# Batch 0's q in four loads instead of two, issued first, in a linear-attention and channel-mix kernel; the written order of all pieces is new

## The chip, the cores and the metric

The kernel runs on one core of a Trainium2 chip. The metric is device time in microseconds (us) of one execution. Five engines work side by side, each through its own instruction stream in order: TensorE (PE in the profile, its weight loads PEld), VectorE (DVE), ScalarE (ACT), GpSimd (POOL) and SyncE (SP). POOL and SP here mostly issue DMAs; sixteen DMA engines move the data.

## The reference

Two stages follow each other, with B = 8 batches, H = 8 heads, S = 576 tokens, head size 64, C = 512 channels and F = 1024:

```python
kv = np.einsum('bhsd,bhse->bhde', k, v)          # 64 x 64 for each batch and head
out = np.einsum('bhsd,bhde->bhse', q, kv)
rms = np.sqrt(np.mean(out * out, axis=-1, keepdims=True) + 1e-06)
x = out / rms * g_norm                           # heads side by side: (B, S, C)

x_prev = x shifted by one token (zeros first)
xk = mu_k * x + (1 - mu_k) * x_prev
xr = mu_r * x + (1 - mu_r) * x_prev
k = np.maximum(xk @ w_k, 0)                      # (S, F)
v = k * k @ w_v                                  # (S, C)
return sigmoid(xr @ w_r) * v
```

All inputs and the output are float32 in HBM; the kernel computes in bfloat16 with float32 sums.

## The kernel before, in words

Attention goes batch by batch. For batches 0 and 1 it goes in two halves of four heads (z = 0, 1), which have their own loads and their own kv; from batch 2 on, both halves go together (written 01). Channel mix goes over groups g = 0 to 8 of 512 tokens, which cut across batches: group g needs the batches whose tokens it holds.

The work is cut into pieces. Each piece is a function that issues a few instructions on one engine; the string ORDER (line 16) names every piece once, in the order in which they are issued, and `Plan.emit` runs through it. An engine executes its pieces strictly in that order; semaphores hold a piece back until what it reads is there and until the buffer that it writes is free. Buffers of a kind rotate (for instance 3 for k, v and q each, 4 double banks of PSUM). `@A` and `@D` behind a name choose ACT or DVE where a piece can run on either. The names that matter (b a batch, z a half, i a half of the tokens or of the sequence, g a group):

- `ld.k/v/q b.z`: loads on POOL's queue, which turn float32 into bfloat16 (lines 217 to 230); `ld.wk0/wk1`, `ld.wr`, `ld.wv0/wv1`: the weights (line 252). `ldh.k`, `ldh.v`: k and v of batch 0's first half as float32 on SP's queue (line 236), which `cst` pieces cast.
- `kv b.z` (line 265): k times v on TensorE; `kc`, `ks`, `kd`: copy, a product with a permutation matrix (`perm`) and a second copy, which bring kv into the shape for the next step.
- `tq b.z.i` (line 358): DVE transposes a half of q; `u b.z.i` (line 282): q times kv. In q's tile a row holds 36 tokens, the halves i = 0 and 1 being the first and the last 18 of each row; each `u` piece waits for both transposes of its half of the heads.
- `sq`, `ss`, `rs` (lines 379 to 439): square, mean over a head by a matmul, 1/sqrt; `sp`: SP spreads that over partitions with small DMAs (line 430); `uc`, `mul` scale u; `d`, `mk`, `mr`, `xk`, `xr` form the difference to the token before and the two blends.
- `k g.f`, `relu`, `ksq`, `r g.c`, `sig`, `v g.c.p`, `out`, `st` (lines 454 to 584): the channel mix and the stores. Group 0 starts in quarters, `k0.half i z`.
- `z:512`: a matmul on zeros, which only fills TensorE's time; there are 29 of them and `zz`; 16 and `zz` stand in front of kv0.0.
- `seta`, `setp`, `setb`, `perm`, `ident`, `small`, `tr9`, `cols`: constants and the three small vectors.

A load piece on POOL stands at one place of the order and waits there for its buffer. Loads go out one behind the other, and POOL's rows show waits that pair each load from the ninth on with the landing of the eighth before it.

Of the kernel before, what the change touches and what calls it, by code (L numbers as in the profile page):

```python
# [31 lines left out]
class Plan:  # L32
# [3 lines left out]
    def add(self, name, on, fn, deps=(), bufs=(), also=None):  # L36
        assert name not in self.pieces, name
        p = self.pieces[name] = Piece(name, on, fn, deps, bufs, also)
        return p
# [17 lines left out]
def kernel(  # L57
# [13 lines left out]
    nc = tc.nc  # L71

    B, H, S, HD = q.shape
# [8 lines left out]
    QJ = S // QP  # L82
# [34 lines left out]
    add = plan.add  # L117

    def get(buf, dtype=None):
        if buf.t is None:  # L120
            n, shape, dt = BUFS[buf.tag]
            pool = psum if buf.tag == "ps" else sb
            buf.t = pool.tile(list(shape), dt, tag=buf.tag, name=buf.tag, bufs=n)
        return buf.t
# [24 lines left out]
    cols = const.tile([128, 9], FP32, name="cols")  # L149
    ones = const.tile([128, 128], BF16, name="ones")  # L150
    heads = const.tile([128, 32], BF16, name="heads")
    perm = const.tile([128, 2, 2, 128], BF16, name="perm")
# [8 lines left out]
    kvq = {(n, b): Buf(n) for n in "kvq" for b in range(B)}  # L161
# [37 lines left out]
    def make_cols(_):  # L199
# [12 lines left out]
                deps=[p_ident, p_small], bufs=[ps9])  # L212
    p_cols = add("cols", "D", make_cols, deps=[p_tr9], bufs=[ps9])

    loaded = {}

    def load(b, n, zs):
        def fn(_):
            if n == "q":
                part = slice(64 * zs[0], 64 * zs[-1] + 64)  # L220
                nc.gpsimd.dma_start(out=get(kvq[(n, b)])[part], in_=q[b].rearrange("h s d -> (h s d)").rearrange(  # L221
                    "(p f) -> p f", p=128)[part])
                return
            view = {"k": k, "v": v}[n][b].rearrange("(m e) (p j) d -> (e p) m (j d)", e=2, j=NJ)
            m = slice(2 * zs[0], 2 * zs[-1] + 2)
            nc.gpsimd.dma_start(out=get(kvq[(n, b)])[:, m, :], in_=view[:, m, :])  # L226

        p = add(f"ld.{n}{b}." + "".join(map(str, zs)), "P", fn, bufs=[kvq[(n, b)]])
        for z in zs:
            loaded[(n, b, z)] = [p]  # L230
# [101 lines left out]
    def attention(b):  # L332
        kin, vin, qin = (kvq[(m, b)] for m in ("k", "v", "q"))
        kv, qT = Buf("kv"), Buf("qT")
        bufs = [{t: Buf(t) for t in ("uT", "sq", "rs", "d")} for z in range(NZ)]
# [4 lines left out]
        for zs in zss:  # L340
# [12 lines left out]
            for i in range(2):  # L353
                def tq(_, i=i, part=part):
                    src = qin.t.bitcast(FP32).rearrange("q (a b i) -> q a b i", b=2, i=32)
                    dst = get(qT).rearrange("q a p b r -> q (a p b r)").bitcast(FP32).rearrange("q (a p b) -> q a b p", p=32, b=2)
                    js = slice(QJ // 4 * i, QJ // 4 * i + QJ // 4)
                    nc.vector.transpose(out=dst[part, js], in_=src[part, js])  # L358

                ts.append(add(f"tq{name}.{i}", "D", tq, deps=sum((loaded[("q", b, z)] for z in zs), []), bufs=[qin, qT]))  # L360
            for z in zs:
                qd[z], kvcs[z] = ts, c
        us = [[Buf("ps") for i in range(2)] for z in range(NZ)]
# [259 lines left out]
```

## Time and profile before

| | us |
|---|---|
| median of the 3 timed runs | 199.68 (199.62 to 199.98) |
| the profiled execution | 200.13 |
| its span | 198.4 |
| TensorE busy | 188.4 |
| DVE busy | 137.8 |
| ACT busy | 121.8 |
| last matmul ends | 194.4 |

The span is what the profile covers of the profiled execution; its own time is 1.7 us more. In the timeline a row has a start, a duration, the engine, the line of the kernel, the instruction, what it writes and reads, and how many were merged; in brackets stands how long the engine had been idle before and what ended that. In the rows of DMA queues q0 is the queue of POOL's loads and q1 that of SP; a row has packets, MB and the share of sixteen engines. MB and KB of POOL's loads are counted in bfloat16, as written.

### The profile page before, as it was taken

The numbers are of one execution on the slowest core, as the hardware profiler recorded it, in microseconds if no ns is written. First come the engines' busy times: TensorE is split into PE (matmuls) and PEld (weight loads), VectorE is DVE, ScalarE is ACT, GpSimd is POOL, SyncE is SP. The second block draws the span as 40 slices with busy tenths as digits, with TensorE's granted clock in tenths as the row PEclk, the third lists the DMA queues.
The fourth block names the chain that finished last, engine by engine and source line by source line (L and its number), as shares of the span: only waits on it lengthen the run. The fifth ranks groups of instructions, "written<-read, shape, count | busy, mean of one in ns | idle before, by whom it ended". The sixth has DMA issues, their size and how long they took to land.

```text
span 198.4 us, 4225 instructions
## 1 busy us (share of the span) xinstructions
PE 188.4 (95%) x1735; PEld 93.3 (47%) x1760; DVE 137.8 (69%) x235; ACT 121.8 (61%) x158; POOL 23.7 (12%) x42
## 2 busy tenths in 40 slices
PE   7889989999999999999999999999999999999992
PEld 2445844443544544444358644444444444444451
DVE  2669998897959968998968497899659421520641
ACT  3365499949976689945778986882219840433410
POOL 7743442141313010000000000000000000000000
PEclk9999999999999999999999999999999999999998
DMA  6999999999999999999703511743213000310444
GB/s 223 191 202 214 204 201 207 214 206 216 206 235 264 216 235 272 260 240 256 210 3 88 175 72 56 220 112 78 45 47 111 2 3 0 140 71 0 153 167 160
DMA packets 21032, 30.63 MB, mean 154 GB/s; under 512 B 1932, under 2 KB 14484, under 8 KB 21012
## 3 DMA queue, kind: packets, MB, share of 16 engines
q0 software_dynamic: 11280, 16.19, 45.7%
q1 hardware_dynamic: 9588, 14.03, 22.2%
q8 instruction: 14, 0.23, 0.4%
q10 hardware_dynamic: 144, 0.13, 0.2%
q14 instruction: 6, 0.05, 0.1%
HBM read 33.56 MB, written 9.44 MB: 217 GB/s over the span
## 4 chain that ended last, share of the span: by engine, by line
PE 68%; DMA 26%; POOL 2%; issue 2%; DVE 0%; POOLq 0%
PE ps L554 27%; PE ps L507 24%; DMA v<-in_v_dram 19%; PE ps L534 12%; DMA w_v<-in_moe_w_v_dram 7%; PE ps L282 2%; PE ps L265 1%; PE ps L388 1%; POOL w_k L252 1%; POOL q L221 1%; PE ps L271 0%; POOL k L226 0%; POOL perm L189 0%; POOL v L226 0%; DVE out L581 0%
## 5 line engine op out<-in xcount | busy, mean ns | idle before, releaser
L554 PE MATMUL ps<-w_v,sqk 128*128 128x512 bf16 (+1 forms) x286 | 65.7, 373 | 0.9 <-issue 0.6
L507 PE MATMUL ps<-xk,w_k 128*128 128x512 bf16 (+1 forms) x280 | 58.1, 355 | 1.1 <-issue 0.8
L465 ACT ACTIVATE relu<-ps 128x1024 bf16<-128x1024 f32 x36 | 36.5, 1026 | 32.5 <-PE ps L507 28.8
L554 PEld LDWEIGHTS <-sqk 128*128 128x128 bf16 x296 | 27.8, 98 | 32.2 <-issue 2.5
L507 PEld LDWEIGHTS <-w_k 128*128 128x128 bf16 x288 | 27.5, 98 | 26.7 <-issue 1.4
L567 DVE TENSOR_TENSOR out<-ps,sig 128x1024 f32<-128x1024 f32 x16 | 19.4, 1221 | 21.9 <-PE ps L554 12.5
L534 PE MATMUL ps<-w_r,xr 128*128 128x512 bf16 x139 | 33.6, 379 | 0.3
L522 DVE TENSOR_TENSOR sqk<-relu 128x1024 bf16<-128x1024 bf16 x32 | 21.2, 684 | 10.0 <-ACT relu L465 9.7
L544 ACT ACTIVATE sig<-ps 128x1024 bf16<-128x1024 f32 x18 | 18.2, 1024 | 12.4 <-PE ps L534 11.5
L534 PEld LDWEIGHTS <-xr 128*128 128x128 bf16 x144 | 13.9, 98 | 16.3 <-issue 0.5
L379 ACT ACTIVATE sq<-ps 128x576 bf16<-128x576 f32 x32 | 19.9, 652 | 1.8 <-PE ps L282 1.5
L358 DVE STREAM_TRANSPOSE qT<-q 128x576 f32<-128x576 f32 (+1 forms) x20 | 14.7, 760 | 2.4 <-DMA q<-in_q_dram 2.3
L144 ACT ACT_TABLE_LOAD x12 | 15.4, 1283 | 0.9 <-PEq L607 0.7
L136 DVE TENSOR_SCALAR uT<-ps,cols 128x576 bf16<-128x576 f32 x13 | 10.4, 816 | 7.7 <-ACT sq L379 5.5
L136 DVE TENSOR_SCALAR md<-d,cols 128x576 bf16<-128x576 bf16 x44 | 13.8, 365 | 0.4
L134 ACT ACTIVATE uT<-ps,cols 128x576 bf16<-128x576 f32 x15 | 10.9, 742 | 2.9 <-PE ps L282 2.9
L300 DVE TENSOR_TENSOR d<-xT 128x1152 bf16<-128x1152 bf16 (+1 forms) x18 | 12.3, 689 | 0.4
L313 DVE TENSOR_TENSOR xr<-md,xT 128x1152 bf16<-128x1152 bf16 x14 | 10.4, 750 | 1.6 <-ACT md L134 1.4
L405 DVE TENSOR_TENSOR xT<-uT,rs 128x1152 bf16<-128x1152 bf16 x14 | 10.4, 750 | 1.1 <-ACT rs L288 0.6
L313 DVE TENSOR_TENSOR xk<-md,xT 128x1152 bf16<-128x1152 bf16 x14 | 10.4, 754 | 0.6 <-ACT md L134 0.4
L450 PE MATMUL ps<-zero 128*128 128x512 bf16 x28 | 9.4, 481 | 1.5 <-DVE zero L164 1.2
L282 PE MATMUL ps<-qT,kv 32*64 32x288 bf16 x256 | 8.5, 290 | 0.8 <-DVE qT L358 0.8
(53 smaller groups left out, 120.9 us busy)
## 6 DMA issues: line engine op xcount, KB each, us to landing
out_dram<-out SPq DMA_DIRECT2D x35, 256.0 KB, 2.3
v<-in_v_dram POOLq DMA_DIRECT2D x6, 576.0 KB, 22.9
k<-in_k_dram POOLq DMA_DIRECT2D x6, 576.0 KB, 23.2
q<-in_q_dram POOLq DMA_DIRECT2D x6, 576.0 KB, 25.5
rs<-rsc SPq DMA_DIRECT2D x48, 72.0 KB, 3.2
q<-in_q_dram POOLq DMA_DIRECT2D x4, 288.0 KB, 10.3
w_k<-in_moe_w_k_dram POOLq DMA_DIRECT2D x2, 512.0 KB, 11.4
w_v<-in_moe_w_v_dram POOLq DMA_DIRECT2D x2, 512.0 KB, 13.8
```

Of the source, the lines that this page charges most:

```text
L136: nc.vector.tensor_scalar(out=dst, in0=src, scalar1=col, scalar2=None, op0=ALU.mult)
L144: nc.scalar.preload_act_table_set(name)
L313: nc.vector.tensor_tensor(out=dst[:, 2 * z:2 * z + 2, r0:r0 + w], in0=md.t[:, :, cs], in1=xT[:, :, cur], op=ALU.add)
L358: nc.vector.transpose(out=dst[part, js], in_=src[part, js])
L379: sq_ = add("sq" + name, "A", lambda _, ps=ps, sq=sq, cs=cs, w=w: nc.scalar.activation(out=get(sq)[:, :, cs], in_=ps.t[:, :, 0:w], func=AF ...
L465: nc.scalar.activation(out=get(rt), in_=ps.t, func=AF.Relu)
L507: nc.tensor.matmul(get(ps)[:, fc % 2, a0:a1], w_k_sb[:, cc, 128 * fc:128 * fc + 128], xk[:, cc, x0:x0 + a1 - a0], start=(cc == 0), stop=(c ...
L522: nc.vector.tensor_mul(out=get(sqk)[:, 2 * f2:2 * f2 + 2, :], in0=rt.t, in1=rt.t)
L534: nc.tensor.matmul(get(ps)[:, ci % 2, :], xr[:, cc, n0:n0 + 128], w_r_sb[:, cc, :], start=(cc == 0), stop=(cc == NHP - 1))
L544: nc.scalar.activation(out=get(sg), in_=ps.t, func=AF.Sigmoid)
L554: nc.tensor.matmul(get(ps)[:, bank, cs], sqk.t[:, fc, 128 * ci:128 * ci + 128], w_v_sb[:, fc, cs], start=(fc == 0), stop=(fc == NFC - 1))
L567: dv = add(f"out{g}.{c2}", "D", lambda _, ps=ps, sg=sg, ot=ot: nc.vector.tensor_mul(out=get(ot), in0=ps.t, in1=sg.t), deps=ms + [sg_done], ...
```

## The change

Batch 0's two loads of q (one for each half of the heads) become four: `ld.q0.z` brings the first 18 tokens of each row and `ld.q0.zb` the last 18. Each transpose of batch 0 waits for the load of its own half alone. q0.0, q0.0b and q0.1b are the first loads, ahead of `perm` and `ident`; q0.1 follows k of the second half. The whole order is new, with 34 pieces on another engine; the number of pieces is otherwise the same.

The order is one line in the code; it is wrapped here and cut to the start, the stretch with the later loads, the place around kv7.01, and the end:

```diff
-ldh.k ldh.v seta setp perm ld.q0.0 ld.q0.1 ld.v0.1 ld.k0.1 ld.wk0 ident ld.wk1 ld.v1.1 ld.k1.1 ld.q1.1 ld.wr ld.q1.0 ld.v1.0 ld.k1.0 ld.wv0 ld.wv1
-ld.v2.01 ld.k2.01 ld.q2.01 table small zz cst.k0@D cst.k1@A setb cst.v0@A cst.v1@D tq0.0.1 tq0.0.0 z:512 z:512 z:512 z:512 z:512 z:512 z:512 z:512
-z:512 z:512 z:512 z:512 z:512 z:512 z:512 z:512 kv0.0 tq0.1.0 kc0.0@A z:512 z:512 ks0.0 tr9 cols kd0.0@A u0.0.0 sq0.00 z:512 z:512 z:512 ss0.00 u0.0.1
-rs0.00 mul0.00 d0.00 tq0.1.1 z:512 z:512 kv0.1 ld.k3.01 ld.v3.01 ld.q3.01 sq0.01 kc0.1@A ss0.01 rs0.01 ks0.1 kd0.1@A z:512 z:512 z:512 u0.1.0 sq0.10
-xk0.00 z:512 z:512 z:512 ss0.10 mul0.01 d0.01 xk0.01 rs0.10 mul0.10 d0.10 u0.1.1 k0.000 sq0.11 ss0.11 rs0.11 k0.110 xk0.10 k0.100 mul0.11 k0.001 d0.11
-xk0.11 relu0.00 xr0.11 xr0.00 k0.010 k0.011 kv1.1 ksq0.00 k0.111 kc1.1@A tq1.1.0 tq1.1.1 ks1.1 xr0.10 relu0.01 kd1.1@A relu0.11 ksq0.11 k0.101 xr0.01
-u1.1.1 uc1.11@A sq1.11 u1.1.0 sq1.10 uc1.10@D relu0.10 ksq0.10 r0.0 r0.1 ss1.2 ss1.3 rs1.2 rs1.3 mul1.1 kv1.0 ld.k5.01 ld.v5.01 kc1.0@D tq1.0.1
-tq1.0.0 r0.2 r0.3 sig0.0 ks1.0 kd1.0@A ksq0.01 sig0.1 v0.0.0 u1.0.1 uc1.01@D u1.0.0 v0.1.0 sq1.00 sq1.01 uc1.00@D v0.1.1 d1.1 ss1.1 rs1.1 v0.0.1
-out0.0 ss1.0 rs1.0 v0.2.0 v0.2.1 mul1.0 d1.0 mk1.0@D xk1.0 v0.3.0 v0.3.1 out0.1 mk1.1@A kv2.01
...
+ldh.k ldh.v ld.q0.0 ld.q0.0b ld.q0.1b seta setp ident perm ld.k0.1 ld.q0.1 ld.v0.1 ld.wk0 ld.v1.1 ld.wk1 ld.k1.1 ld.q1.1 ld.k1.0 ld.v1.0 ld.wr ld.q1.0
+ld.wv0 ld.wv1 ld.k2.01 ld.v2.01 ld.q2.01 table small zz setb cst.k0@D cst.v0@D cst.k1@A cst.v1@A z:512 z:512 z:512 z:512 z:512 z:512 z:512 z:512 z:512
+z:512 z:512 z:512 z:512 z:512 z:512 z:512 kv0.0 kc0.0@A z:512 z:512 ks0.0 kd0.0@A tq0.0.0 tq0.0.1 z:512 z:512 u0.0.1 u0.0.0 tr9 sq0.00 cols tq0.1.1
+z:512 z:512 ss0.00 tq0.1.0 rs0.00 mul0.00 d0.00 xk0.00 z:512 z:512 z:512 z:512 kv0.1 ld.k3.01 ld.v3.01 ld.q3.01 sq0.01 ss0.01 kc0.1@A rs0.01 ks0.1
+kd0.1@A z:512 z:512 z:512 u0.1.0 sq0.10 u0.1.1 sq0.11 k0.000 mul0.01 d0.01 xk0.01 xr0.01 ss0.10 rs0.10 mul0.10 d0.10 xk0.10 ss0.11 rs0.11 mul0.11
+k0.010 k0.100 k0.001 relu0.00 k0.011 relu0.01 d0.11 xk0.11 xr0.11 kv1.1 kc1.1@D k0.101 ks1.1 kd1.1@A tq1.1.0 tq1.1.1 relu0.10 k0.110 u1.1.0 ksq0.00
+u1.1.1 sq1.10 xr0.10 uc1.11@A kv1.0 ld.k5.01 ld.v5.01 kc1.0@A uc1.10@D sq1.11 xr0.00 tq1.0.0 k0.111 relu0.11 ss1.3 rs1.3 tq1.0.1 ss1.2 ks1.0 ksq0.11
+r0.2 r0.3 rs1.2 r0.0 mul1.1 kd1.0@A u1.0.1 u1.0.0 sig0.1 sq1.00 r0.1 ksq0.10 sq1.01 uc1.01@A sig0.0 v0.1.0 d1.1 ksq0.01 v0.0.0 v0.0.1 mk1.1@D xk1.1
+ss1.1 uc1.00@D v0.1.1 out0.0 rs1.1 ss1.0 rs1.0 v0.3.0 v0.3.1 v0.2.0 v0.2.1 mul1.0 d1.0 mk1.0@D kv2.01
...
```

From kv2.01 to kv4.01:

```diff
-kv2.01 ld.v4.01 ld.k4.01 ld.q4.01 xk1.1 kc2.01@A mr1.1@A k1.0.0 k1.1.0 ks2.01 k1.2.0 k1.3.0 k1.2.1 kd2.01@A tq2.01.1 tq2.01.0 ld.q6.01 k1.3.1 relu1.1
-k1.0.1 u2.01.1 sq2.11 mr1.0@D k1.1.1 uc2.01@D k1.6.0 k1.7.0 k1.6.1 relu1.0 uc2.11@D u2.01.0 sq2.01 sq2.10 sq2.00 uc2.10@D k1.7.1 k1.4.0 k1.5.0 xr1.1
-k1.4.1 uc2.00@A ss2 kv3.01 ld.k7.01 ld.v7.01 xr1.0 rs2 ksq1.0 kc3.01@D relu1.3 tq3.01.0 tq3.01.1 ld.q5.01 k1.5.1 relu1.2 ksq1.3 r1.0 ks3.01 kd3.01@A
-r1.2 ksq1.1 ksq1.2 r1.1 sig1.0 r1.3 sig1.1 u3.01.0 sq3.00 v1.2.0 uc3.00@D v1.3.0 v1.2.1 sq3.10 u3.01.1 uc3.11@A uc3.10@D kv5.01 ld.k6.01 ld.v6.01
-sq3.11 kc5.01@A v1.3.1 v1.1.0 ks5.01 kd5.01@A v1.1.1 uc3.01@A v1.0.0 sq3.01 ss3 v1.0.1 sp2.0 sp2.1 rs3 st0.0 mul2.0 d2.0 mk2.0@D xk2.0 mul2.1 d2.1
-mk2.1@D st0.1 sp3.0 mr2.0@A xk2.1 k2.2 sp3.1 out1.0 k2.3 out1.1 st1.3 k2.0 kv4.01
...
+kv2.01 ld.k4.01 ld.v4.01 ld.q4.01 kc2.01@A xk1.0 k1.0.0 k1.6.0 mr1.0@A out0.1 k1.7.0 k1.6.1 ks2.01 kd2.01@A tq2.01.0 tq2.01.1 ld.q5.01 k1.7.1 xr1.0
+relu1.3 k1.1.0 k1.0.1 u2.01.1 sq2.11 uc2.01@D k1.2.0 k1.1.1 uc2.11@D sq2.01 relu1.0 k1.3.0 mr1.1@D xr1.1 k1.2.1 u2.01.0 sq2.00 k1.3.1 uc2.00@D ksq1.3
+k1.4.0 k1.5.0 sq2.10 tq3.01.0 relu1.1 ksq1.1 tq3.01.1 k1.4.1 ksq1.0 ss2 rs2 uc2.10@A sp2.1 k1.5.1 relu1.2 r1.2 kv3.01 ld.v6.01 ld.k7.01 ld.q6.01
+kc3.01@A r1.0 r1.3 sig1.1 ks3.01 kd3.01@D ksq1.2 r1.1 sig1.0 v1.1.0 u3.01.1 sq3.11 uc3.11@D sq3.01 v1.0.0 sp2.0 uc3.01@A v1.1.1 u3.01.0 sq3.10 sq3.00
+v1.3.0 uc3.00@A v1.0.1 mul2.1 st0.3 uc3.10@A v1.2.0 kv5.01 ld.k6.01 ld.v7.01 ss3 d2.1 mk2.1@D xk2.1 v1.3.1 mul2.0 d2.0 st0.2 rs3 sp3.0 v1.2.1 mk2.0@D
+xk2.0 kc5.01@A mr2.0@A sp3.1 mr2.1@A ks5.01 kd5.01@D k2.4 k2.5 out1.1 st1.2 xr2.0 k2.2 relu2.2 k2.0 k2.1 ksq2.2 xr2.1 relu2.0 kv4.01
...
```

Around the same amount of TensorE work in both, before and after:

```diff
-r3.2 r3.3 xk4.1 tq6.01.1 sig3.1 v3.2.0 u5.01.1 uc5.01@A v3.2.1
...
+u5.01.1 uc5.11@A uc5.01@A out2.0 st2.0 xr3.0 st2.1 sq5.01 k3.6 k3.7 st1.1 sq5.11 k3.0 relu3.3 st1.0 ksq3.1 u5.01.0 uc5.10@A sq5.10 tq6.01.1 k3.1
+relu3.0 st2.3 r3.0 ksq3.3 r3.1 sig3.0 k3.4 ksq3.0 k3.5 v3.0.0 kv7.01 relu3.2 uc5.00@D kv6.01 sq5.00 ss5 kc6.01@A mul4.1 d4.1 mk4.1@D rs5 v3.1.0
+kc7.01@A ksq3.2 v3.1.1
...
```

The end, and the code:

```diff
-v8.0.10 out8.00 v8.3.00 v8.3.10 out8.30 st8.00 st8.30 v8.3.01 v8.3.11 out8.31 st8.31
+v8.0.10 out8.00 st8.00 v8.2.10 out8.20 st8.20 v8.1.10 out8.10 st8.10 v8.3.01 v8.3.11 out8.31 st8.31 v8.3.00 v8.3.10 out8.30 st8.30
```

```diff
@@ -225,6 +225,15 @@
             m = slice(2 * zs[0], 2 * zs[-1] + 2)
             nc.gpsimd.dma_start(out=get(kvq[(n, b)])[:, m, :], in_=view[:, m, :])
 
+        if n == "q" and not b:
+            def half(_, i):
+                rows_ = slice(64 * zs[0], 64 * zs[0] + 64)
+                src, fs = q[b].rearrange("h s d -> (h s d)").rearrange("(p f) -> p f", p=128), slice(QJ // 2 * HD * i, QJ // 2 * HD * (i + 1))
+                nc.gpsimd.dma_start(out=get(kvq[(n, b)])[rows_, fs], in_=src[rows_, fs])
+
+            loaded[(n, b, zs[0])] = [add(f"ld.{n}{b}.{zs[0]}{x}", "P", lambda _, i=i: half(_, i), bufs=[kvq[(n, b)]])
+                                 for i, x in enumerate(("", "b"))]
+            return
         p = add(f"ld.{n}{b}." + "".join(map(str, zs)), "P", fn, bufs=[kvq[(n, b)]])
         for z in zs:
             loaded[(n, b, z)] = [p]
@@ -357,7 +366,8 @@
                     js = slice(QJ // 4 * i, QJ // 4 * i + QJ // 4)
                     nc.vector.transpose(out=dst[part, js], in_=src[part, js])
 
-                ts.append(add(f"tq{name}.{i}", "D", tq, deps=sum((loaded[("q", b, z)] for z in zs), []), bufs=[qin, qT]))
+                ts.append(add(f"tq{name}.{i}", "D", tq, deps=sum((loaded[("q", b, z)][0 if b else i:][:1] for z in zs), []),
+                              bufs=[qin, qT]))
             for z in zs:
                 qd[z], kvcs[z] = ts, c
         us = [[Buf("ps") for i in range(2)] for z in range(NZ)]
```

## The prediction

> **What bounds the kernel now.** First the page's busy line and its DMA slices, then the TensorE timeline, the issues on POOL with their landing times, and the two DMA queues in short windows.
>
> ```profile
> PE 188.4 (95%) x1735; PEld 93.3 (47%) x1760; DVE 137.8 (69%) x235; ACT 121.8 (61%) x158; POOL 23.7 (12%) x42
> ...
> DMA  6999999999999999999703511743213000310444
> ```
>
> TensorE works without a real gap from about 17 us to its end at 194.40, and the DMA engines are full until about 98 us: the loads of all eight batches stand in one long queue. So there are two clocks to beat, TensorE's sum of matmuls and the arrival of the loads. The timeline shows where they meet:
>
> ```profile
> 9.82 0.44 PE L282 MATMUL ps<-qT,kv 32*64 32x288 bf16 x8 [0.59 <-DVE qT L358]
> ...
> 12.74 0.76 PE L265 MATMUL ps<-v,k 64*64 64x64 bf16 x36 [0.42 <-ACT sq L379]
> ...
> 40.67 0.78 PE L265 MATMUL ps<-v,k 64*64 64x64 bf16 x72
> ...
> 58.89 0.77 PE L265 MATMUL ps<-v,k 64*64 64x64 bf16 x72 [0.35 <-DMA v<-in_v_dram]
> ...
> 94.71 1.03 PE L554 MATMUL ps<-w_v,sqk 128*128 128x512 bf16 x4
> ...
> 101.82 0.78 PE L265 MATMUL ps<-v,k 64*64 64x64 bf16 x72
> ```
>
> In order these are u0.0.0, kv0.1, kv2.01, kv5.01, v3.2.0 and kv6.01 (in the same view kv0.0 starts at 7.29 and k0.000 at 17.01). kv5.01 waits openly for a load. The last loads are issued and land thus (the last column of a load's own line is us from issue to landing):
>
> ```profile
> 59.99 0.74 POOL L226 DMA_DIRECT2D k<-in_k_dram  x1 [4.24 <-PE ps L265]
> ...
> 63.53 0.82 POOL L226 DMA_DIRECT2D v<-in_v_dram  x1 [2.80 <-DMA v<-in_v_dram]
> ...
> v<-in_v_dram POOLq DMA_DIRECT2D x1, 576.0 KB, 31.6
> ...
> q<-in_q_dram POOLq DMA_DIRECT2D x1, 576.0 KB, 26.6
> ```
>
> The second-last load, issued at 63.53, lands at 95.1; q7, issued at 71.97, at 98.6. Before, nothing on TensorE asks for that second-last load until 101.82.
>
> **The change part by part, from the profiled execution (200.13 us, span 198.4; 0.45 above the median of the timed runs, 199.68).**
>
> *Issues.* POOL now waits 1.08 us for the zeroed perm and spends 0.82 on it before the first q, at 2.32. After, three q pieces come first, at about 0.75 (SP and ACT start at 0.74). A q issue took 0.54 us for 288 KB and for 576 KB, so I take 0.54 for a half: three make 1.6, then ident and perm 1.0, so perm is ready at about 3.4; its first reader, ks0.0, runs at 8.51. The two extra issues (1.1 us of POOL) are hidden: each later load waits for the landing of the eighth load before it (the waits named in POOL's rows pair off so), with eight in the queue.
>
> *Landings.* The loads land in issue order. Issue plus time to landing gives the old landings, which I carry over by the bytes up to each load's end: 8.3 us at 0.29 MB (q0.0, 2.32 + 6.0), 9.8 at 0.59, 11.2 at 0.88, 12.75 at 1.18 (k0.1, 4.24 + 8.5), 15.2 at 1.70, 19.4 at 2.52. kv0.1 needed k0.1 as the fourth load, 12.75; now it needs v0.1, with the same bytes before it: 12.75 again. wk1 goes from 18.35 to 19.4, wr from 24.8 to 28.4 (r0.2 comes at about 29). Half of q0.0 should land at about 7.4, the other at 8.4.
>
> *u of the first half.* u0.0.0 waited 0.59 for the transposes (two of 0.75 from 8.34). Now the transposes end near 9.1, and kd0.0 (8.96 + 0.37) binds: u may start at 9.4. But u0.0.1 is put first (0.36), so u0.0.0 ends at 10.15 against 10.26: gain 0.1. mul0.00 stays at 12.1 to 12.2.
>
> *DVE.* setb (1.0 us) moves into DVE's 3.05 us of idle before k lands. tq0.1.0 and tq0.1.1 go into DVE's 1.41 us of idle before mul0.00; tq0.1.0 waits for q0.1 (11.2), with mul0.00 queued behind it, which isn't ready before 12.1 anyway. mul0.01 moves from 15.24 to about 14.5. There xr0.01 (0.95) is put ahead of mul0.10, which waits for ss0.10, now behind k0.000: xk0.10 ends at about 20.0 (before: 19.82).
>
> *TensorE to kv1.1.* kv0.1 to u0.1.0 took 2.37 us (12.74 to 15.11) and still does; u0.1.1 follows with no zeros between, so k0.000 starts at 15.6 to 15.9, not 17.01. Then two ss and two more k0 pieces (0.91 each, 4.57/5) end at 19.1, and k0.001 waits for xk0.10 until 20.0. Its head start of 1.3 is thus mostly idle: with two more k0 pieces kv1.1 comes at 21.9, one k0 piece poorer than before at 22.90. Gain 0.1.
>
> *To kv2.01.* The same pieces precede kv2.01 in both orders. Its later load (v2 now, k2 before) is the seventeenth by bytes and landed at 40.6, so it cannot start before 40.7: nothing gained. For a loss I take 0 to 0.5 (kc1.1 on DVE now stands behind xr0.11).
>
> *40 to 94 us.* TensorE's busy time in windows of 10 us was 9.60, 9.01, 9.84, 9.95, 9.95; 9.95 is what a full one shows, so 1.4 us of idle lies here. The new order puts more in front of kv5.01 (3.5 us, less v1.2.1 at 0.9), so the wait for v5 goes. I credit none to all of the 1.4. One new wait lies here: tq3.01.0 is put ahead of ksq1.1 and ksq1.0 on DVE, which gets there near 50 and waits for q3 (29.74 + 22.1 = 51.85); v1.1.0 on TensorE reads those products, ready at 54.7 (two transposes and two products of 0.7 each); TensorE gets there at 54.1 (13.4 us of matmuls behind 40.7): 0 to 0.6, inside that idle.
>
> *kv7.01, where it ends up.* The pieces ahead of kv7.01 after are those ahead of v3.2.0 before, plus u5.01.0, u5.01.1 (0.38 each) and v3.0.0 (0.86), minus r3.2 and r3.3 (0.86 each): 0.1 less. So at the old pace kv7.01 comes at 94.6, and up to 1.4 earlier if the idle goes. It needs v7, now the second-last load, with the same 0.59 MB behind it: 95.1, and 0.2 from landing to matmul as at kv5.01 (34.52 + 24.2 = 58.7, started 58.89): 95.3. TensorE stops for 0.7 to 2 us, and whatever was won earlier goes into that wait. Queued behind it are kv6.01 (its k6 is earlier, at 90.1), ss5 and v3.1.0; ACT waits for ss5 and kv6.01, DVE has the blends of batch 4 to do. What lies behind it is the same amount: 194.40 - 94.6 = 99.8 us with 0.5 of idle in it. The stores ahead of this point are eleven in both, so I see no reason for another landing; bounds 94.4 and 96.3, since about 0.45 MB of stores moved after 95 us.
>
> *Engines swapped.* 34 pieces change between DVE and ACT (DVE 40 to 36, ACT 40 to 44). A blend product costs 1.43 as a pair on ACT and 0.65 on DVE. Cover: both have idle in every 10 us beyond 100 but one (DVE 9.75 at 130 to 140). Without it one pair costs 0.8; bounds -0.5 (the idle left behind kv7.01) to +0.8; I take 0. *Tail:* the last store goes out on SP instead of ACT; SP's of that size landed in 1.8 us; -0.2 to +0.2, taken 0.
>
> Sum: 95.3 - 94.6 = +0.7, span 199.1, profiled execution 200.85, against the median 200.4.
>
> **The unknown at the start.** Do the earlier q pieces delay k and v of batch 0, on the other queue? Windows 4.5 to 5.0 and 5.0 to 5.5:
>
> ```profile
> q1 hardware_dynamic: 88, 0.19, 98.3%
> q0 software_dynamic: 2, 0.01, 10.5%
> ...
> q0 software_dynamic: 17, 0.08, 90.5%
> q1 hardware_dynamic: 61, 0.08, 42.1%
> ```
>
> q's first packets run 2.2 to 2.7 us after the issue, just when k and v end. Now they could run from about 3.0 to 3.4, with 0.7 MB of k and v still to move. Other rows show how a newcomer fares, between 50 and 96 us with loads and behind 100 without:
>
> ```profile
> out_dram<-out SPq DMA_DIRECT2D x11, 256.0 KB, 7.8
> ...
> rs<-rsc SPq DMA_DIRECT2D x24, 72.0 KB, 6.1
> ...
> out_dram<-out SPq DMA_DIRECT2D x24, 256.0 KB, 2.1
> ...
> rs<-rsc SPq DMA_DIRECT2D x24, 72.0 KB, 2.1
> ```
>
> Even 72 KB waits 4 us behind what the engines hold of the other queue. So k and v, there first, should go first: 0. The other end, equal turns: 1.7 us of k and v take twice that, v lands 1.6 later, kv0.0 at 8.9, ss0.00 and its four zeros push kv0.1 to 13.9, and kv2.01 is 1.2 late. The nearest row is rs, so I take 0 and keep 1.2.
>
> The Trainium skill, "DMA: Bandwidth & Descriptors", section "Queues, rings and completion order", says the opposite: an engine takes turns between queue rows, a whole packet of descriptors at a time. By it the sum would go by equal turns, to 200.9 at most. The 4 us of the rs rows speak against short turns.
>
> **Rivals.** *A, the wait at kv7.01:* +0.7, 200.4 (200.1 to 200.9), 0.45. *B, equal turns at the start:* 1.2 late at kv2.01; if the 1.4 of idle behind it takes nothing up, kv7.01 comes at 95.8, behind v7: 200.9; with a stall of an engine swapped, 201.7. For it: q's early readiness; against: rs. 0.20. It is the case for the skill's rule. *C, faster:* v7 lands before TensorE asks. This decides at a landing of 94.4: if the store traffic goes behind it so that it lands at 93.6, kv7.01 starts at 93.8, and 0.8 of the old idle is kept: 198.9. For: 1.4 of idle is there to win; against: a full DMA queue with the same bytes. 0.17. *D, no change:* landing near 94.8 or the later idle won back: 199.7, 0.18. That the two transposes still wait for both halves (the change not doing what it says) moves u0.0.1 by nothing, since kd0.0 binds.
>
> **Numbers.** Likeliest A: 200.4. 0.2% (0.4 us) is about what a measurement can tell. Faster is C, 0.17; same is D and the edge of A, 0.20; slower is B and the rest of A, 0.63. The range 199.2 to 201.6 leaves out the far half of C and the end of B.
>
> **What would show it.** Right: a wait on a DMA of v in front of kv7.01 near 95 us; kv2.01 at 40.7 to 41.2; u0.0.1 near 9.4; k0.001 idle before 20. Wrong: kv0.0 clearly behind 7.3 (B); kv7.01 without a wait, or v7 landing before 94.4 (C).

## The result and the profile after

The changed kernel takes 199.39 us (median of 21 runs, 199.08 to 199.91) against 199.74 us before on the same chip (21 runs, 199.42 to 200.55): a ratio of 0.998, 95% interval 0.9971 to 0.9989. It is about 0.35 us faster, where 0.7 us slower was forecast. Two more measurements on other chips gave 0.9983 (0.9971 to 0.9995) and 0.9992 (0.998 to 1.0005). The profiled execution took 199.39 us with a span of 197.5, against 200.13 and 198.4 before.

The busy line and the DMA slices of the page after. TensorE has the same work and the same share, DVE is 3.8 us lighter and ScalarE 5.2 us heavier than before, as the swapped pieces say.

```profile
PE 188.0 (95%) x1736; PEld 93.2 (47%) x1760; DVE 134.0 (68%) x227; ACT 127.0 (64%) x166; POOL 24.6 (12%) x44
...
DMA  6999999999999999999632404413506003002226
```

The TensorE timeline after (start, us, engine, line, operands; in brackets the idle time in front and what ended it). Lines of the code stand 9 or 10 further down than before: L274 is kv, L291 u, L418 ss, L492 k0, L517 k.

```profile
7.24 0.76 PE L274 MATMUL ps<-v,k 64*64 64x64 bf16 x36
...
9.34 0.69 PE L291 MATMUL ps<-qT,kv 32*64 32x288 bf16 x16
...
12.01 0.76 PE L274 MATMUL ps<-v,k 64*64 64x64 bf16 x36
...
17.37 0.41 PE L418 MATMUL ps<-sq,ones 128*128 128x288 bf16 x2 [0.83 <-ACT rs L297]
18.25 3.65 PE L492 MATMUL ps<-xk,w_k 128*128 128x256 bf16 x32 [0.48 <-DVE xT L411]
...
40.00 0.78 PE L274 MATMUL ps<-v,k 64*64 64x64 bf16 x72
...
60.07 0.78 PE L274 MATMUL ps<-v,k 64*64 64x64 bf16 x72
63.96 4.49 PE L517 MATMUL ps<-xk,w_k 128*128 128x512 bf16 x20 [0.70 <-DVE xk L322]
...
94.27 1.53 PE L274 MATMUL ps<-v,k 64*64 64x64 bf16 x144
```

These are kv0.0, both u of the first half, kv0.1, ss0.11, a run of k0 pieces, kv2.01, kv5.01, k2.4 and, last, kv7.01 with kv6.01. Two things differ from the forecast. kv0.1 and kv2.01 come 0.73 and 0.67 us earlier than before (12.74 and 40.67). And the row of kv7.01, where the forecast put a wait of 0.7 us, names no wait at all. POOL's issue of v7 and its time to landing, after:

```profile
62.60 0.80 POOL L226 DMA_DIRECT2D v<-in_v_dram  x1 [0.69 <-DMA k<-in_k_dram]
...
v<-in_v_dram POOLq DMA_DIRECT2D x1, 576.0 KB, 28.5
```

It lands at 62.60 + 28.5 = 91.1, not at 95.1, 3.2 us before TensorE asks. From the start of kv0.0 to the end of the last matmul TensorE takes 186.58 us (7.24 to 193.82), before 187.11 (7.29 to 194.40).

### The profile page after: what moved, and what is told of

Its sections match the earlier page's. It is cut to its first block, busy times and chain, and to the rows that moved or that the text cites. A ratio compares the mean times of both kernels' runs of the same rounds, so it can differ in the third digit from the quotient of the medians.

```text
span 197.5 us, 4233 instructions
## 1 busy us (share of the span) xinstructions
PE 188.0 (95%) x1736; PEld 93.2 (47%) x1760; DVE 134.0 (68%) x227; ACT 127.0 (64%) x166; POOL 24.6 (12%) x44
## 4 chain that ended last, share of the span: by engine, by line
PE 73%; DMA 14%; DVE 6%; ACT 2%; issue 2%; SPq 1%; POOL 0%; DVEq 0%; ACTq 0%
PE ps L517 25%; PE ps L564 25%; PE ps L544 12%; DMA q<-in_q_dram 11%; PE ps L460 4%; DMA rs<-rsc 3%; PE ps L492 2%; PE ps L291 2%; PE ps L274 2%; DVE xT L411 1%; DVE qT L367 1%; ACT relu L475 1%; DVE xk L329 1%; DVE d L309 1%; PE ps L398 1%
## 5 line engine op out<-in xcount | busy, mean ns | idle before, releaser
L517 PE MATMUL ps<-xk,w_k 128*128 128x512 bf16 (+1 forms) x280 | 59.1, 355 | 1.4 <-DVE xk L322 0.7
L564 PEld LDWEIGHTS <-sqk 128*128 128x128 bf16 x296 | 28.3, 98 | 32.6 <-issue 1.8
L517 PEld LDWEIGHTS <-w_k 128*128 128x128 bf16 x288 | 27.2, 98 | 27.9 <-issue 1.8
L134 ACT ACTIVATE md<-d,cols 128x576 bf16<-128x576 bf16 x20 | 14.2, 769 | 1.7 <-DVE d L309 1.5
L134 ACT ACTIVATE uT<-ps,cols 128x576 bf16<-128x576 f32 x16 | 11.7, 744 | 1.2 <-PE ps L291 1.2
L136 DVE TENSOR_SCALAR md<-d,cols 128x576 bf16<-128x576 bf16 x36 | 11.3, 363 | 0.2
L136 DVE TENSOR_SCALAR uT<-ps,cols 128x576 bf16<-128x576 f32 x12 | 9.6, 814 | 2.7 <-ACT sq L389 2.5
```

The source lines that it names most:

```text
L134: nc.scalar.mul(out=dst, in_=src, mul=col)
L136: nc.vector.tensor_scalar(out=dst, in0=src, scalar1=col, scalar2=None, op0=ALU.mult)
L517: nc.tensor.matmul(get(ps)[:, fc % 2, a0:a1], w_k_sb[:, cc, 128 * fc:128 * fc + 128], xk[:, cc, x0:x0 + a1 - a0], start=(cc == 0), stop=(c ...
L564: nc.tensor.matmul(get(ps)[:, bank, cs], sqk.t[:, fc, 128 * ci:128 * ci + 128], w_v_sb[:, fc, cs], start=(fc == 0), stop=(fc == NFC - 1))
```

## Experiments

The change has three parts: q's first load in **halves**, the **issue** of q ahead of perm, and the new **order** of all later pieces. The first experiments do or undo them one at a time. One table behind them puts all ratios together.

### The halves alone, in the old order

```diff
-... seta setp perm ld.q0.0 ld.q0.1 ld.v0.1 ...
+... seta setp perm ld.q0.0 ld.q0.0b ld.q0.1 ld.q0.1b ld.v0.1 ...
```

> The order of before, with each of batch 0's two q loads replaced in its place by its two halves; each transpose waits for its own half. Theory packets (the halves, with rows of half the size, stream faster, and that alone brings every later load earlier): k0.1 lands at 11.6 to 12.0 instead of 12.75, kv0.1 starts near 12.0, the later load of kv2.01 lands at 39.6 to 40.0 instead of 40.6, and the time is 0.2 to 0.5 us below before. Theory issue (it is the issue ahead of perm that brings the loads earlier): landings as before, 12.75 and 40.6, time within 0.1 of before. Theory order (the loads matter little, the new order of the pieces wins): landings may move, the time does not.

Measured 199.56 us (12 runs) against 199.84, 0.9992 (0.9974 to 1.0011): not told from no change. The loads land as before (k0.1 at 12.8, the later load for kv2.01 at 40.6). u0.0.0 comes at 9.09 without its wait of 0.59, and kv0.1 then waits 1.19 us for k0.1. The halves do what they say, and the gain stops at the next landing.

### The new order and the early issue, with whole loads

```diff
-... ld.q0.0 ld.q0.0b ld.q0.1b seta setp ident perm ld.k0.1 ld.q0.1 ld.v0.1 ...
+... ld.q0.0 seta setp ident perm ld.k0.1 ld.q0.1 ld.v0.1 ...
```

The edit also moves the second half of q0.1 from ahead of k0.1 to behind it.

> The changed order, with q of batch 0 as two whole loads: q0.0 first, q0.1 whole behind k0.1. Theory packets: v0.1 lands at 12.5 to 12.8 again, v2 at 40.4 to 40.8, the gain is gone or reversed: 0.0 to +0.5 us against before. Theory issue: v0.1 at 11.6, as fast as the change (-0.35). Theory order: as fast as the change whatever the landings.

> The order of the change with two whole loads of q for batch 0, again, beside the change on one chip. Its landings were those of the change (v2 40.0, v7 91.3), its median 0.7 us above that of the change, its profile 0.5 us late from kv0.0 on. Theory 'halves': the whole first load is needed for both transposes, lands 0.5 to 1.1 us later than the halves, and the first u products and all behind them start later: 200.0 to 200.3, with u0.0.1 more than 0.3 us later behind kv0.0 than in the change. Theory 'execution': the 0.7 came from a late start of the full TensorE rate alone: median within 0.2 us of the change's in the same call.

Measured 200.21 us (12 runs; 199.84 before), 1.0017 (1.0002 to 1.0032), and beside the change on another chip 200.63 (5 runs) against 199.61 for the change and 199.86 before, 1.0041 (1.0029 to 1.0053). So the theory that only the execution differed falls. The landings are those of the change within 0.5 us (v2 at 40.0, v7 at 91.3 and 91.0), so it isn't the halves that bring the later loads forward. The u of the first half start 2.31 us behind kv0.0 in the second profile, 2.10 in the change: 0.21 later, less than the 0.3 expected of "halves"; in the first profile it is 2.10 too. Nor does the loss lie clearly at a later wait: the idle time near 64 us is 0.93 and 1.25 (0.70 to 0.99 in three profiles of the change), and the last matmul ends at 194.4 and 194.5 (193.8 to 194.4). What stands clear is the end: from the last matmul to the end of the span both profiles have 4.2 us, the change 3.7. "The tail" comes back to it.

### The halves and the new order, with q behind perm

```diff
-... ld.q0.0 ld.q0.0b ld.q0.1b seta setp ident perm ld.k0.1 ...
+... seta setp perm ld.q0.0 ld.q0.0b ld.q0.1b ident ld.k0.1 ...
```

> The changed kernel, with perm issued ahead of q's loads again, so that q goes out at about 2.3 instead of 1.24. Theory packets: q's first packets run near 5.0 in both cases, behind k and v of the other queue, so landings and time are those of the change (-0.35 against before). Theory issue: the landings fall back by 0.5 to 1 us and the time to that of before.

> The changed kernel with seta, setp and perm ahead of the three early pieces of q on GpSimd, as the kernel before has them, again, since the first profile of it fell into a disturbed execution. Theory 'issue ahead of perm brings all loads forward': q is issued near 2.3 and not 1.2, each later landing is as before (kv0.1 near 12.7, the later load for kv2.01 40.6, v7 0.4 or more behind 91.1), time 0.8 to 1.5 above the change. Theory 'order': landings and time as the change, within 0.3.

The first measurement gave 201.28 us, 1.0065 (1.0036 to 1.0095), the second 200.58 (8 runs), 1.0053 (1.0032 to 1.0074), 0.97 above the change measured beside it. Its TensorE timeline shows where:

```profile
6.92 0.76 PE L274 MATMUL ps<-v,k 64*64 64x64 bf16 x36
...
13.35 0.75 PE L274 MATMUL ps<-v,k 64*64 64x64 bf16 x36 [1.62 <-DMA v<-in_v_dram]
```

kv0.1 waits 1.62 us for v0.1, which lands at 13.2 (11.6 in the change). An issue 1.1 us later at the very start thus comes with 1 us more at the end. The DMA windows from 7 to 8 and from 8 to 9 us, when only the software queue has work, say what happened to the stream. First the change, then this kernel:

```profile
q0 software_dynamic: 157, 0.20, 113.1%
q0 software_dynamic: 175, 0.21, 120.5%
```

```profile
q0 software_dynamic: 91, 0.14, 97.2%
q0 software_dynamic: 139, 0.16, 101.2%
```

0.41 MB against 0.30 in these two microseconds. In both kernels the queue's first bytes come at about 5 us, but with the earlier issue 0.11 MB more arrive, half a microsecond of the stream at its 0.22 MB per us; the landings further on are 0.7 to 1.2 us apart (the later load for kv2.01 at 39.6 and 39.7 in two profiles of the change, 40.4 here; v7 at 91.1 and 91.4, and 92.3). Over all profiles it is 0.37 to 0.43 MB with the early issue and 0.30 to 0.36 without. Why the stream is thin just there, with POOL's loads already issued, no row shows.

### Early issue in the old order, without and with halves

```diff
-... seta setp perm ld.q0.0 ld.q0.1 ld.v0.1 ...
+... ld.q0.0 ld.q0.1 seta setp perm ld.v0.1 ...
```

> The kernel before with its two whole loads of q for batch 0 moved ahead of seta, setp and perm, and nothing else. Theory 'issue': the software queue stands 0.1 MB further by 10 us as in the change, kv0.1 comes 0.4 to 0.7 earlier and the later load for kv2.01 lands at 40.0 in place of 40.6; in this order, with its 1.4 us of idle time between 40 and 94, the time moves by -0.6 to 0. Theory 'order': the lead needs the change's order of the loads too, and landings and time stay within 0.2 of before (199.85).

```diff
-... seta setp perm ld.q0.0 ld.q0.1 ld.v0.1 ...
+... ld.q0.0 ld.q0.0b ld.q0.1 ld.q0.1b seta setp perm ld.v0.1 ...
```

> The kernel before with all four halves of q for batch 0 ahead of seta, setp and perm: both parts of the change without the new order of the pieces. If halves and early issue each bring their part in the old order as well, 0.3 (the halves in place, 199.56) and up to 0.6 more: 199.0 to 199.6. If the new order is what makes use of them, no faster than the halves alone: 199.5 to 199.9.

> Early issue and halves in the old order again, beside the change. Theory 'order loses': 0.3 to 0.6 under the change in the same call, about 199.05 when before is 199.75. Theory 'order is even': within 0.2 of the change.

The whole loads gave 199.64 us (12 runs) against 199.73, 0.9996 (0.9986 to 1.0006). The landings do come forward, as "issue" expected (kv0.1 12.05, the later load for kv2.01 at 39.7, not 40.6), but the time hardly follows (kv0.0 came at 7.53 there, before at 7.29). With the halves as well the kernel takes 199.05 (0.9968, 0.9955 to 0.9981) and, beside the change, 199.19 (0.997, 0.996 to 0.998) against 199.63 for the change. Both parts in the old order beat the whole change by 0.44 us on one chip. All the waits over 0.2 us on TensorE in that second profile:

```profile
7.37 0.76 PE L274 MATMUL ps<-v,k 64*64 64x64 bf16 x36 [0.72 <-ACT v L128]
12.74 0.76 PE L274 MATMUL ps<-v,k 64*64 64x64 bf16 x36 [0.78 <-DMA k<-in_k_dram]
29.22 0.41 PE L418 MATMUL ps<-sq,ones 128*128 128x288 bf16 x2 [0.43 <-DVE uT L136]
```

Behind kv0.0 that is 1.21 us. The change, measured beside it, has 0.22, 0.83, 0.49 and 0.99, together 2.53, of which 1.32 are the two waits near 18 us and 0.99 the wait at 64.61, places where the old order has none. TensorE from kv0.0 to its end: 186.32 us here (7.37 to 193.69), 186.77 in the change (7.59 to 194.36). That is 0.45 apart, a third of the difference in these waits; the rest was not traced. Nor is the start of this profile early: k0.1 lands at 12.74, as before the change, where the first profile of the same kernel has it at 11.74.

### The new order alone

```diff
-... ld.q0.0 ld.q0.0b ld.q0.1b seta setp ident perm ld.k0.1 ...
+... seta setp perm ld.q0.0 ident ld.k0.1 ...
```

Here q's two loads are whole again, the second behind the load of k for the second half.

> The new order of the pieces without the other two parts: two whole loads of q for batch 0, the first behind seta, setp and perm as in the kernel before, the second behind the load of k for the second half. Theory 'order loses': the new order without early issue and halves is slower than before by the sum of what each of them brought in it, 0.6 to 1.0 (halves) and 1.0 (issue): 201.0 to 201.8. Theory 'order wins by itself': 199.2 to 199.7.

> The change beside the two others: 0.3 to 0.4 under before, as in both measurements so far. It is the reference of this call.

Measured 200.78 us (6 runs) against 199.76 before and 199.63 for the change; 1.0055 (1.0041 to 1.0069). "Order loses" is right, though the size was below its range: the parts don't add. All ratios to before, each with its interval:

| | old order | new order |
|---|---|---|
| whole loads, behind perm | 1 | 1.0055 (1.0041-1.0069) |
| halves, behind perm | 0.9992 (0.9974-1.0011) | 1.0065 (1.0036-1.0095), 1.0053 (1.0032-1.0074) |
| whole loads, ahead of perm | 0.9996 (0.9986-1.0006) | 1.0017 (1.0002-1.0032), 1.0041 (1.0029-1.0053) |
| halves, ahead of perm | 0.9968 (0.9955-0.9981), 0.997 (0.996-0.998) | 0.998 (0.9971-0.9989), 0.9983 (0.9971-0.9995), 0.9992 (0.998-1.0005) (the change) |

The new order by itself costs 1 us, halves and early issue together win 1.2 to 1.5 in it and 0.6 in the old one. In the old order neither does much without the other; in the new order the early issue alone brings 0.3 to 0.8, the halves alone nothing (1.0065 and 1.0053 beside 1.0055).

The profiles, one for each measurement, show the two parts in two places. The early issue moves the end of the last matmul: in the old order from 194.4 and 194.6 to between 193.5 and 193.8, in the new order from about 195.0 in both to between 193.8 and 194.5. The halves go with a shorter end behind it: 3.4 to 3.7 us in all eleven profiles with halves, 4.0 to 4.2 in all five with whole loads, in either order. So of what the halves add to an early issue, 0.6 us in the old order and about 1 in the new, half a microsecond lies behind the last matmul, where the theories of these runs didn't look.

### Who decides when v7 lands

Stores and loads share the DMA engines, as the windows below show. SP's rows of before, then of after:

```profile
71.52 3.46 SPq L456 DMA_DIRECT2D out_dram<-out  x5
82.15 5.03 SPq L430 DMA_DIRECT2D rs<-rsc  x8
87.28 3.54 SPq L456 DMA_DIRECT2D out_dram<-out  x4
```

```profile
68.49 4.25 SPq L466 DMA_DIRECT2D out_dram<-out  x4
84.42 5.69 SPq L440 DMA_DIRECT2D rs<-rsc  x8
90.21 4.49 SPq L466 DMA_DIRECT2D out_dram<-out  x5
```

Before, nine stores go out between 71.5 and 90.8 us. After, four go out by 72.7, and the other five only from 90.21 on, since they stand behind the spreads of batch 4 in SP's queue, for which SP waits 11.3 us until ScalarE has their input. The test moves three of them back ahead of those spreads in the changed kernel:

```diff
-... out1.0 ksq2.1 st1.3 ... out2.1 ss4 rs4 ... sp4.1 sp4.0 ... st1.1 ... st1.0 ... st2.3 ...
+... out1.0 ksq2.1 st1.3 st1.1 st1.0 ... out2.1 st2.3 ss4 rs4 ... sp4.1 sp4.0 ...
```

> The changed kernel with three quarter stores of mixes 1 and 2 moved ahead of the two spreads of batch 4 on SP, so that seven stores and not four go out near 68 to 75, as against four or five in the kernel before. Theory 'bytes shared': each store takes 0.262 MB from a stream of 0.22 MB per us that both queues share, so the load of v for batch 7 lands up to 3.6 us later than 91.1, 93 to 94.7, all later loads too, and kv7.01 (94.27 in the change) waits 0 to 0.5: time plus 0 to 0.5. Theory 'issue': the landing is set by when GpSimd issues and by the order of the loads alone: 91.1 within 0.5, time as the change.

SP's row of the stores, v7's issue and its time to landing:

```profile
69.12 14.57 SPq L466 DMA_DIRECT2D out_dram<-out  x7
...
62.77 0.75 POOL L226 DMA_DIRECT2D v<-in_v_dram  x1
...
v<-in_v_dram POOLq DMA_DIRECT2D x1, 576.0 KB, 31.1
```

The seven stores are out by 83.7. v7 lands at 62.77 + 31.1 = 93.9, as "bytes shared" said, against 91.1 in the first profile of the change and 91.4 in the one measured beside this kernel. The queues from 75 to 90 us, in the change, then with the stores ahead, then before (packets, MB, share):

```profile
q0 software_dynamic: 1776, 2.50, 93.0%
q1 hardware_dynamic: 664, 1.06, 22.0%
```

```profile
q0 software_dynamic: 1465, 2.06, 76.3%
q1 hardware_dynamic: 1042, 1.81, 36.7%
```

```profile
q0 software_dynamic: 1445, 2.04, 75.2%
q1 hardware_dynamic: 1238, 1.80, 38.3%
```

0.75 MB more of stores took 0.44 MB from the loads, and the load queue is back where it was before. In order_alone, with the change's stores but neither halves nor early issue, v7 landed at 91.8; in the old order with both, at 94.7 and 95.0. So it is the place of the stores more than the start of the stream that moved this landing: the test gives back 2.5 to 2.8 of the 4.0 us. The remaining 1.3 us was not tested by itself; the early issue has a part in it, since in the new order without it v7 landed 0.9 to 1.0 later than in the change measured beside it (91.8 after 90.8, 92.3 after 91.4). The time stayed that of the change, 199.54 (12 runs), 0.9985 (0.9974 to 0.9997): 93.9 is still ahead of TensorE, which came to kv7.01 at 95.19 in a profile whose kv0.0 came 0.87 us later than in the first one of the change.

### What a wait at kv7.01 costs

On top of the last edit, v7 is made the last load:

```diff
-... kv5.01 ld.k6.01 ld.v7.01 ... ld.q7.01 ...
+... kv5.01 ld.k6.01 ... ld.q7.01 ld.v7.01 ...
```

> stores_ahead, and the load of v for batch 7 issued behind that of q for batch 7, so that it is the last load. In stores_ahead the last load landed at 97.2, when TensorE reached kv7.01 at 95.2 (94.3 in the change). Theory 'a wait here costs one for one', which the prediction used: v7 lands at 97 to 97.5, kv7.01 waits 2 to 3 us behind its landing and cast, and the time is 2 to 3 above that of stores_ahead (199.5): 201.5 to 202.5. Theory 'absorbed': TensorE's later idle time or the tail gives part of it back, less than 1.5 us in time.

```profile
68.49 0.78 PE L274 MATMUL ps<-v,k 64*64 64x64 bf16 x72
...
98.03 1.42 PE L274 MATMUL ps<-v,k 64*64 64x64 bf16 x144 [3.57 <-DMA v<-in_v_dram]
```

kv7.01 waits 3.57 us for a landing at 97.9, more than the 2 to 3 expected, and the time is 203.5 us (4 runs, 202.49 to 204.08), 1.0187 (1.0157 to 1.0217), 4.0 above stores_ahead. From kv0.0 to the last matmul it is 190.5 us against 186.5 in stores_ahead. Nothing behind 98 us gives the wait back: the mechanism of the forecast is real, a wait here costs about what it lasts.

### The tail

> The changed kernel, with the last two quarter stores in the old sequence, so that the last one goes out on ACT's queue. If the end of the span behind the last matmul (4.0 us before, 3.7 after) is set by the queue of the last store, the time is 0.2 to 0.3 us above the change, near before; if that difference is chance, there is none.

With the last two quarter stores in the old sequence the changed kernel took 199.53 us (12 runs), 0.9984 (0.9972 to 0.9997): no difference. The time from the last matmul to the end of the span is 3.7 in both, 4.0 before. What it does follow is the loads of q: 4.0 to 4.2 in the five profiles with whole loads, 3.4 to 3.7 in the eleven with halves, whichever queue has the last store. In each of the five, and in none of the eleven, the DMA rows show a packet of the instruction queue (q14) at the very end of the span. No run tests whether that packet, or anything else that two more load pieces move in the program, makes the end longer.

### Faster than both: the spreads on two queues

The new wait at 64 us hangs on spreads that SP issues one by one. In the changed kernel, two of the four that mul2.1 needs go out on ScalarE:

```diff
-                nc.sync.dma_start(out=get(rs)[64 * e:64 * e + 64, y, :],
+                (nc.scalar if e and (b, z) == (2, 1) else nc.sync).dma_start(out=get(rs)[64 * e:64 * e + 64, y, :],
```

> The changed kernel with two of the four spreads that mul2.1 waits for issued by ScalarE and not by SP. In the change mul2.1 starts at 57.92 behind these DMAs, issued 0.74 us apart from 49.73 on, and the chain from it lets TensorE wait 0.70 at 63.96. Theory 'the issue on SP sets it': mul2.1 starts 0.7 to 1.4 earlier, the idle time at 64 is gone, time 0 to 0.7 under the change (199.5). Theory 'the transfers beside the loads set it': mul2.1 moves by less than 0.3, and the 1.5 us of ScalarE at 50 cost 0 to 0.7.

Measured 198.9 us (7 runs) against 199.73 before, 0.9962 (0.9948 to 0.9976); the change, which wasn't measured beside it, has 0.998 to 0.9992. The idle time at 64 is gone. DVE's row of mul2.1, in the other profile of the change whose kv0.0 starts at the same time (7.70), and then here (7.72):

```profile
58.40 0.76 DVE L415 TENSOR_TENSOR xT<-uT,rs 128x1152 bf16<-128x1152 bf16 x1 [1.14 <-DMA rs<-rsc]
```

```profile
57.93 0.76 DVE L415 TENSOR_TENSOR xT<-uT,rs 128x1152 bf16<-128x1152 bf16 x1 [0.41 <-DMA rs<-rsc]
```

It starts 0.47 us earlier, less than the 0.7 to 1.4 of "the issue on SP sets it", and kv4.01 follows 0.47 earlier (68.38 against 68.85); kv5.01 is 0.26 later. This kernel and the one with the early halves in the old order are the fastest run; the spreads on two queues together with the old order weren't run.

### The change again

> The change itself, beside the other kernels of this call on one chip. All theories: about 0.35 us (0.2%) under the kernel before; the load of v for batch 7 lands near 91.1, kv2.01 starts near 40.0, kv0.1 near 12.0. In the other profiles the start of full TensorE rate differed between executions and moved kv0.0 within 7.0 to 7.7; this run shows whether the same kernel does that too: theory 'start varies' has kv0.0 off 7.24 by up to 0.4 with no edit at all, its rival 'start belongs to the kernel' has 7.24 again within 0.1.

199.61 us (11 runs), 0.9983. kv0.0 starts at 7.70, in the first profile of the very same kernel at 7.24: "start varies" holds, with 0.46 where up to 0.4 was expected.

## Why the prediction was wrong

**The step that failed is "kv7.01, where it ends up"**, and in it one sentence: "The stores ahead of this point are eleven in both, so I see no reason for another landing." The count is right and says nothing, because what matters is when they go: five of the eleven were sent from 90.21 on, behind spreads that wait for batch 4. The landing moved from 95.1 to 91.1, far outside the bounds of 94.4 to 96.3, and stores_ahead shows that the place of the stores made 2.5 to 2.8 us of that. TensorE found v7 there and did not stop: the term of +0.7, the whole of the forecast's sum, measured 0. The rest of the step holds: TensorE came there at 94.27 (94.6 forecast), and late_v7 shows that a wait there costs about what it lasts. The span was 197.5 and not 199.1: 0.7 of the 1.6 is this wait, 0.3 the earlier arrival at kv7.01, 0.25 the stretch behind it, 0.3 the tail. It is rival C's mechanism, with a landing even before its 93.6; the gain is smaller than its 198.9, since kv7.01 came at 94.27 and not at 93.8.

**Landings carried over by bytes**: too late by 0.4 (wk1) to 1.15 (v0.1). v0.1 landed at 11.6, not 12.75, the later load for kv2.01 at 39.6, not 40.6, so kv2.01 came at 40.00 where "it cannot start before 40.7" was written. A landing isn't a function of the bytes ahead alone: q_behind_perm2 and early_q_old_order show that the earlier issue moves the stream. In the twelve profiles with q issued early the later load for kv2.01 lands at 39.5 to 40.0, in the four with q behind perm at 40.4 to 40.6. Nearer to the start the landings scatter more: kv0.1's load lands at 11.6 to 12.7 in the twelve, at 12.7 to 13.2 in the four. *Issues*: q went out at 1.24, not 0.75, behind 0.80 of POOL's own queue, and perm was ready at 3.98, not 3.4; both hidden, as said.

**The u of the first half** was right: u at 9.34 (9.4), mul0.00 at 12.11 (12.1 to 12.2). **TensorE to kv1.1** was right in sum: kv1.1 at 21.84 (21.9), a gain of 0.15 (0.1) after the piece that is missing. The idle time lies in two waits near 18 us, not in one before 20.

**40 to 94 us**, "I credit none", was right: TensorE is busy 53.29 us of the 55 from 40 to 95 before (9.60, 9.01, 9.84, 24.84) and 53.41 after (9.79, 9.89, 8.99, 24.74). The wait for v5 went, as forecast. The wait that took its place was not the one named, q3 at tq3.01.0 (DVE waited 1.91 us there, TensorE did not stop for it), but the one for the spreads at 63.96, which the prediction didn't look at.

**Engines swapped and tail**: from kv7.01 to the last matmul 99.55 us (99.8 forecast), inside the bounds. The tail gave 0.3, a little outside its 0.2, and old_tail shows it isn't the last stores' sequence; it goes with the halves, a step that the prediction didn't have.

**Rival B, equal turns at the start**, was not seen in the change's profile: v's cast begins at 6.00 (6.22 before). In the twelve profiles with q issued early it begins at 5.89 to 7.59, with a median of 6.47, in the four with q behind perm at 6.22 to 6.34. So the usual delay is far from the 1.6 of equal turns, but the early issue goes with a wider scatter, and one execution (7.59) came within 0.3 us of it; a small delay can't be excluded. The windows of after from 4.5 to 5.0 and from 5.0 to 5.5:

```profile
q1 hardware_dynamic: 85, 0.20, 98.8%
q0 software_dynamic: 1, 0.00, 2.4%
...
q0 software_dynamic: 31, 0.07, 76.0%
q1 hardware_dynamic: 55, 0.08, 46.0%
```

Up to 5.0 us q0 had moved a single packet, though its first load was issued at 1.24. By the rule in the Trainium skill, "DMA: Bandwidth & Descriptors", section "Queues, rings and completion order", an engine with work in two queues alternates between them; the trace doesn't show that at the start, and no run tells whether q waited for k and v or for its own descriptors. In q_behind_perm2 q was issued 1.07 us later and also started at about 5 us, which speaks for the first, but is no test of it. Between 75 and 90 us the two queues do share, in the numbers above.

## To carry to other kernels

When two queues share the DMA engines, a load's landing depends on when the other queue's transfers go, so look for the wait that stands in front of those stores on their own queue; counting them is not enough. Judge a new order together with what it was searched for: here it costs 1 us by itself and is worth having only with the landings that the early issue brings, and the two small edits in the old order do better. Before a microsecond is explained, look at how far the same kernel's start moves between executions.

## What the runs showed of the hardware beyond that

The start of a kernel is not fixed. Nine of TensorE's zeros, from the same 4.58 us on, took 2.25 us in one execution and 3.23 in another. The rows are of old_tail, then of whole_new_order:

```profile
4.58 2.25 PE L460 MATMUL ps<-zero 128*128 128x512 bf16 x9
```

```profile
4.58 3.23 PE L450 MATMUL ps<-zero 128*128 128x512 bf16 x9
```

Single zeros are 0.43 us apart at first and 0.22 later, and the change of pace came between 4.15 and 6.7 us over the sixteen profiles, in the change itself at 5.85, 6.6 and 6.7, while the clock row of the profile's page shows 90% or more in that stretch. The Trainium skill, "TensorE: Matmul & The Clock Gate", section "What's actually happening", has TensorE at half rate for its first 3.4 us or so, with a window that runs freely, so that the moment varies; the trace agrees that the moment varies, but here it comes 3.0 to 5.5 us after the first zero, in twelve of sixteen profiles later than 3.4. With v's landing, which varies as well, this puts kv0.0 anywhere from 6.92 to 8.11 us, and in the change itself at 7.24, 7.59 and 7.70. That is more than the whole effect of the change, so two profiles can be compared from kv0.0 on, and times by their medians.
